# Square of the GELU argument written back to the matmul's PSUM bank, with the next VectorE step reading it there

## Chip, cores and metric

One core of one Trainium2 chip. The metric is the device time of one execution in microseconds (us). Lower is better. A trace covers one profiled execution, and its span runs from the first to the last instruction, about 1.7 us less than the device time. Each execution has a state: fast, or slow, where the granted clock or the time shows a disturbed run.

Engines: PE is TensorE's matmuls, PEld its weight loads, DVE VectorE, ACT ScalarE, POOL GpSimd, SP the engine that issues most DMAs.

## The reference, cut to what matters

```python
def reference(...):
    g = sigmoid((x * gate_w).sum(-1))              # gate
    a = A_ref(x, wq, wk, wv, wo, beta)             # attention in 4 segments, 16 heads, with a memory;
                                                   # beta goes through a sigmoid too
    b = B_ref(x, w1, b1, w2, b2)                   # layer norm, then an MLP over the token axis
    return g * a + (1 - g) * b

def B_ref(x, w1, b1, w2, b2):                      # x: 1 x 2048 x 448
    h = layernorm(x)
    u = einsum('bsd,sf->bdf', h, w1) + b1          # f = 1792
    u = gelu(u, approximate=True)                  # 0.5 u (1 + tanh(sqrt(2/pi) (u + 0.044715 u^3)))
    y = einsum('bdf,fs->bds', u, w2) + b2
    return y.transpose(0, 2, 1)
```

## The kernel before

The kernel builds a list of operations with their reads and writes, and five texts give the order of each engine. Waits follow from the two. `name:n` in the text stands for n consecutive matmuls of a group, `name=4` for the PSUM bank that the group takes. Banks 0 to 3 belong to the attention scores. Banks 4 to 7 rotate among all other matmul groups. A group gets its bank when every operation that names it in `buse(b)` has run.

The first MLP matmul makes 14 tiles of 128 x 448, each followed by five steps:

```python
# mm1(ft), the tile ft, scratch half q = ft % 2
op("PE", ...)            # 16 matmuls into bank b, named u{ft}-0 .. u{ft}-15
op("ACT", lambda e: e.activation(gg[:, q, :], bank(b)[:, 0:D], ACT.Square, bias=b1s[:, ft : ft + 1],
                                 scale=math.sqrt(GC)),
   **buse(b), reads=[bres(b), R_bias], writes=[R_gg[q]], name=f"gsq{ft}", ...)      # GC u^2
op("ACT", lambda e: e.activation(vh[:, q, :], bank(b)[:, 0:D], ACT.Identity, bias=b1h[:, ft : ft + 1], scale=0.5),
   **buse(b), reads=[bres(b), R_bias], writes=[R_vh[q]], name=f"gvh{ft}", ...       # u/2, on ACT or DVE
op("DVE", lambda e: e.scalar_tensor_tensor(gg[:, q, :], gg[:, q, :], 1.0, vh[:, q, :], op0=ALU.add, op1=ALU.mult),
   reads=[R_gg[q], R_vh[q]], writes=[R_gg[q]], name=f"garg{ft}", ...)               # (1 + GC u^2) u/2
op("ACT", ... ACT.Tanh on gg[:, q, :] ..., name=f"gth{ft}")
op("DVE", ... (gg + 1) * vh -> uT[:, ft, :] ..., name=f"gelu{ft}")
```

A tile of the full 128-column form is split in four 32-column strips when a stretch between attention groups is short:

```python
def mm(e, out, w, x, split, **kw):
    if not split:
        return e.matmul(out, w, x, ...)
    for q in range(0, 128, 32):
        last = e.matmul(out[q : q + 32], w[:, q : q + 32], x, ...)
    return last
```

The softmax here doesn't subtract the row's maximum and nothing guards it: scores larger than these inputs give would overflow.

Of the kernel before, what the change touches and what calls it, by code (L numbers as in the profile page):

```python
# [5 lines left out]
ACT = mybir.ActivationFunctionType  # L6
ALU = mybir.AluOpType
# [5 lines left out]
D = 448  # L13
# [288 lines left out]
def pool_cost(n):  # L302
# [7 lines left out]
        warm fill0 fill1 fill2 trx1_0=4 trx1_1=5 trx0_0=6 fill3 gtr trx0_1=7 fill4 fill5 v03t v03s v03a v03b v03c  # L310
        k0a=45 v03d k0c k0b=67 q0a k0d q0b q0d q0c v67a=54 sc0_0 v67c k1a=67 k1c sc0_1 k1b=45 k1d q1a=67 sc0_2 q1c
        q1b=45 q1d sc0_3 u0-0=6 u1-0:2=7 u0-1:2 u1-2:2 pv0=4 u0-3 sc0_4 u1-4 u0-4 u1-5 btr=5 u2-0=4 u1-6 u0-5:2 u2-1:2
        u1-7 u3-0=5 u0-7 u3-1 sc1_0 u3-2:2 u2-3 u0-8:2 u2-4 u0-10 u1-8:2 u3-4 u1-10 sc1_1 u0-11 u1-11 u3-5 u1-12
        u0-12:2 u1-13 u0-14 u1-14 u0-15 u2-5 u1-15 u2-6:2 u3-6 u2-8 u3-7:2 sc1_2 u3-9 u5-0=6 u2-9 u3-10:2 u2-10:2 u5-1
        pv1=7 sc1_3 u5-2 u2-12 u5-3 u2-13 u4-0=7 u5-4 u4-1:5 u3-12 u4-6 u2-14:2 u4-7 u5-5 sc1_4 u4-8 u3-13 u4-9 u5-6
        u3-14:2 u5-7:2 u6-0=4 u5-9 u4-10:2 u6-1 u4-12:2 u6-2 u4-14 sc2_0 u7-0=5 u5-10 u4-15 u5-11 u7-1:2 u6-3:2 u7-3
        u5-12:2 u7-4 sc2_1 u7-5 u5-14 u7-6:3 pv2=7 u5-15 u6-5 u7-9 u6-6:3 u7-10 sc2_2 u6-9 mst0=7 u6-10:2 pv3=6 u7-11
        u6-12 u7-12 sc2_3 u7-13 u8-0:2=7 u7-14 u9-0=6 u6-13 u9-1:2 u6-14 u8-2 u7-15 u8-3 sc2_4 u6-15 u8-4 u9-3 u8-5
        u9-4 u8-6:2 u9-5 pv4=5 u9-6 sc3_0 u9-7 u8-8:2 u9-8 u8-10 mem4=4 u9-9 u8-11 u9-10:4 u8-12:2 u9-14:2 u8-14:2
        k2a=45 sc3_1 k2c k2b=67 k2d sc3_2 q2a=54 q2b=67 q2c q2d sc3_3 v96a=45 v96b=67 v96c v96d sc3_4 u11-0:4=4 mem6=5  # L320
        u10-0:3=7 u11-4 u10-3 pv6=6 u10-4 u11-5 pv5=5 sc4_0 u10-5:3 u13-0=5 u10-8 u11-6:2 u10-9 u13-1 mem5=6 u11-8
        u10-10 sc4_1 u10-11:2 u11-9 u10-13 u13-2 u10-14 u11-10 u13-3 u10-15 u11-11:3 u13-4 u11-14:2 u13-5 sc4_2
        u12-0:6=6 pv7=7 u12-6 u13-6 u12-7 sc4_3 mst1=4 u12-8 u13-7:2 mem7=7 u13-9 u12-9 u13-10 u12-10 sc4_4 u13-11
        u12-11 u13-12 u12-12:3 wo2=4 u12-15 wo3=7 u13-13:3 wo0~2=4 wo1=7 sc5_0 k3a=64 k3b=57 k3c k3d sc5_1 v14a=46
        pv8=5 v14c pv9=7 wo5=5 mem9=4 sc5_2 q3a=76 q3b=54 q3c q3d sc5_3 y0-0:5=7 y1-0:2=6 y0-5 y3-0:2=4 y1-2 y3-2:2
        mem8=5 y0-6 y1-3 y3-4 sc5_4 y3-5:2 y0-7 y3-7 y0-8:2 y1-4:2 y3-8:2 y0-10 sc6_0 y3-10 y0-11:2 y3-11 wo4=5 y1-6
        y3-12 y1-7 y0-13 sc6_1 y1-8:2 y3-13 y1-10:2 mem11=5 wo6=7 y1-12:2 y4-0=5 sc6_2 pv11=4 y4-1:2 y2-0=6 y4-3
        y2-1:2 y4-4 pv10=4 y4-5 sc6_3 y2-3 y4-6 y2-4 y4-7:2 mem10=7 y4-9 y5-0:2=4 y2-5:2 sc6_4 y2-7 y5-2 mst2=7 y2-8:2
        y5-3:3 y2-10 y4-10 y5-6 sc7_0 y2-11 y5-7 y2-12 y6-0=7 y5-8:3 y2-13 y6-1 y4-11 y6-2 y5-11 y4-12 sc7_1 y5-12
        y4-13 y6-3 pv12=6 y5-13 wo7=5 sc7_2 y6-4:4 y7-0:4=5 y6-8 mem12=6 y6-9 y7-4:4 mem13=4 y6-10 y7-8:2 sc7_3 pv13=6  # L330
        y6-11:3 wo9=4 y7-10 sc7_4 y7-11:2 mem14=6 y7-13 wo8=4 pv14=7 wo10=6 wo11=5 pv15=4 y8-0:2=7 y9-0:2=5 y8-2
        y9-2:3 mem15=6 y8-3 y9-5:2 y8-4:4 y9-7 y8-8:2 y9-8:2 y11-0=6 y10-0:2=4 y9-10 y11-1 y10-2 y8-10:2 y9-11 y11-2
        y8-12:2 y11-3 y10-3 y9-12:2 y11-4 y10-4 y11-5:2 y10-5 y11-7:2 y10-6:2 y11-9 y10-8 y11-10:2 y10-9:2 y11-12
        y10-11 y11-13 y10-12:2 wo12=7 wo14=6 wo13=4 y13-0=5 wo15=7 y15-0=6 y13-1 y15-1 y13-2:2 y15-2 y13-4:2 y14-0:4=4
        y15-3 y13-6:2 y12-0:2=7 y14-4:3 y12-2 y15-4 y13-8 y14-7 y15-5:2 y14-8 y13-9 y12-3 y14-9:3 y12-4 y13-10 y15-7
        y14-12 y12-5 y13-11 y15-8 y13-12 y15-9:2 y13-13 y12-6:4 y14-13 y15-11 y12-10 y15-12:2 y12-11:3 y15-0~2=5
        y15-1~2 y15-2~2 y15-3~2 y15-4~2 y15-5~2 y15-6~2 y15-7~2 y15-8~2 y15-9~2 y15-10~2 y15-11~2 y15-12~2 y15-13~2
    """,
    "ACT": """
        ldx2 ldwv1 ldwv2 xTcp0_10 xTcp0_00 cpv0 cpv1 cpv2 gt0 gt1 cpv3 gt2 cpk0_0 ek0_0 gt3 cpk0_3 ek0_1 cpk0_2 cpv4  # L340
        cpq0_1 gt4 cpq0_3 tb exp0_0=2 gt7 gt6 cpk1_0 exp0_1=3 cpk1_2 cpq1_3 exp0_2=4 cpq1_1 exp0_3=0 cpv5 gt5 eq1_0
        exp0_4=1 eq1_1 exp1_0=5 ek0_2 exp1_1=6 eq1_2 gsq0 gsq1 ek0_3 exp1_2=2 gth0 exp1_3=3 eq1_3 gth1 gsq2 exp1_4=0
        gsq3 gth2 ek1_1 exp2_0=1 gsq4 gth3 exp2_1=4 gsq5 ek1_0 gvh5 exp2_2=5 gth5 gth4 exp2_3=6 ek1_3 gsq7 exp2_4=0
        gsq6 gth7 gvh6 exp3_0=2 gth6 ek1_2 gsq9 gsq8 gvh8 exp3_1=3 cpk2_0 cpk2_3 cpq2_3 exp3_2=1 cpq2_1 cpv8 gt8
        exp3_3=4 cpv9 gt9 gt10 ek2_1 gt12 gth8 eq2_0 gt11 exp3_4=7 exp4_0=2 gth9 exp4_1=3 eq2_1 gsq10 gsq11 exp4_2=0
        ek2_0 exp4_3=5 gth11 gth10 exp4_4=6 ag2 eq2_3 gsq12 gsq13 gvh12 gvh13 ag1 exp5_0=1 gth12 cpk3_0 cpk3_3 cpq3_3
        exp5_1=4 cpv14 gt14 eq2_2 gt15 ag5 gth13 exp5_2=7 cpq3_0 ek2_3 cpq3_1 gt13 exp5_3=2 ek2_2 eq3_0 exp5_4=3
        exp6_0=0 ag4 eq3_1 exp6_1=5 eq3_2 exp6_2=6 exp6_3=2 exp6_4=3 exp7_0=1 exp7_1=4 ag7 exp7_2=7 eq3_3 exp7_3=0 ag9
        exp7_4=5 ag8 ag11 ag10 ag14
    """,  # L350
    "DVE": """
        ob0 bns2 bns1 xTcp0_11 gw bna1 xTcp0_01 bns0 padk0 padx0 padk1 padx1 bna2 bns3 bna0 padq3 padq1 bna3 padq2
        bns6 cpk0_1 ln1 bns7 bns5 bns4 ln0 bna6 mk0_0 bna4 bna7 cpq0_2 cpq0_0 bna5 bns11 bns15 cpv7 cpv6 ln2 ln3 bns8
        omgh cpk1_1 mk0_1 bna8 ln5 ln4 ln7 cpk1_3 ln6 bns12 bns9 cpq1_0 oc0 bna11 bns10 bna15 cpq1_2 bna12 phk0_0
        bna10 bna9 phk0_1 ta0 bns13 b1c bna13 bns14 b2c mo0 ln9 ln11 bna14 b1h ln8 gcol1 ln10 oc1 rec0 oc2 ln12 ln13
        ln15 ln14 mq1_0 mk0_2 phk0_2 b1s mq1_2 gh gvh0 gvh1 garg1 mk0_3 oc3 mg0 garg0 ta1 phk0_3 gelu0 mq1_1 oa0 rec1
        phq1_1 mo1 gvh2 gelu1 garg2 gcol0 oa1 gvh3 ot0 gelu2 mk1_1 mg1 garg3 phk1_1 gvh4 mo2 mg2 garg4 gelu3 ta2 rec2
        garg5 msta0 mk1_0 oa2 ta3 ot1 gelu5 mq1_3 mo3 gelu4 phk1_0 gvh7 mg3 garg7 phq1_0 mstc0 gelu7 mk1_3 garg6 tm4
        ta4 gelu6 rec3 gvh9 eps4 phq1_2 phk1_3 cpk2_1 rec4 oa3 cpk2_2 om4 oa4 mk1_2 phq1_3 cpq2_0 cpq2_2 ot3 ot2 omg0
        garg8 cpv10 cpv12 cpv11 phk1_2 tm6 mk2_1 eps6 ot4 phk2_1 ta5 ta6 garg9 tm5 gelu9 eps5 gelu8 rec5 gcol2 oa5 om5  # L360
        b2g0 gvh10 rec6 gvh11 mq2_0 om6 garg11 ta7 phq2_0 msta1 omg2 garg10 tm7 gelu11 mq2_1 gelu10 mstc1 omg1 oa6
        eps7 rec7 ag3 ot5 ag0 oa7 b2g1 garg12 phq2_1 mk2_0 om7 cpk3_1 cpk3_2 ot6 ot7 ta8 cpv15 ta9 garg13 tm9 phk2_0
        mq2_2 gelu12 phq2_2 gelu13 eps9 rec9 cpv13 mq2_3 om9 cpq3_2 phq2_3 tm8 eps8 mk2_3 mq3_0 phk2_3 mk2_2 oa9 b2g2
        rec8 om8 phk2_2 fin0 tm11 fin3 fin1 oa8 eps11 ta11 rec11 ag6 ta10 phq3_0 tm10 eps10 rec10 oa11 om10 msta2
        gcol3 ot8 omg3 mq3_1 om11 mq3_2 phq3_1 oa10 phq3_2 fin2 fin4 b2g3 ot9 mstc2 ot10 ta12 ot11 fin5 tm12 tm13
        eps12 rec12 mq3_3 oa12 om12 ta13 fin6 tm14 eps13 fin7 rec13 ta14 oa13 om13 eps14 phq3_3 rec14 ot12 tm15 ta15
        eps15 rec15 oa15 oa14 om14 om15 ot13 fin8 ot15 ot14 fin11 fin10 fin9 ag12 ag13 ag15 fin13 fin14 fin15 fin12
        fin15~2
    """,
    "POOL": """  # L370
        z3_0 id0 id1 mhalf z3_1 v0 v1 padq0 vpe0 rstd0 vpe4 wo0 rstd4 mask0_1_1 maskg0 mask0_0_0 mask0_1_3 mask0_2_2
        mask0_2_2~2 vpe8 mask0_3_0 rstd8 vpe12 rstd12 mask1_1_1 mask0_4_1 mask0_4_3 mask1_0_0 mask1_3_0 mask1_2_2
        mask1_4_1 mask1_2_2~2 mask2_0_0 mask1_1_3 mask2_1_1 mask1_4_3 mask2_1_3 mask2_2_2 mask2_2_2~2 mask3_0_0
        mask2_4_1 mask3_1_1 mask3_2_2 mask2_3_0 mask3_1_3 mask3_2_2~2 o4 mask2_4_3 mask3_4_1 mask3_4_3 mask3_3_0
# [17 lines left out]
def build_kernel(nc, X, WQ, WK, WV, WO, BETA, W1, B1, W2, B2, GW, OUT):  # L392
# [24 lines left out]
    def bank(b):  # L417
        return ps[:, b.bank if isinstance(b, Bank) else b, :]

    def bres(b):  # L420
        return b.res if isinstance(b, Bank) else R_bank[b]
# [4 lines left out]
    def buse(b):  # L426
        return {"use": (b,)} if isinstance(b, Bank) else {}
# [823 lines left out]
```

## Time and profile before

| | kernel before |
|---|---|
| median device time, first 3 runs | 174.0 us (173.86 to 174.17) |
| span of the profiled run | 170.9 us, granted clock 1.000 |
| busy: TensorE / VectorE / ScalarE / GpSimd | 166.1 / 144.2 / 127.0 / 68.6 us |
| whole matmuls recorded / strip matmuls | 404 / 508 |

(The trace has 411 weight loads for the whole matmuls, so 7 of their records are missing.) TensorE is busy to 97%, so the question for any edit elsewhere is whether TensorE waits less. The profiled run of before happened to be a quick one: its device time is 172.65, 1.3 us under the median, so spans are compared only with care.

### The profile page before, as it was taken

What the parts mean: (1) busy time and instruction counts of PE and PEld (TensorE: products, weight loads), DVE (VectorE), ACT (ScalarE), POOL (GpSimd) and SP (SyncE); (2) the same over time, 40 slices, a digit from 0 to 9 for tenths busy, and PEclk for the clock granted to TensorE, in tenths of its full rate; (3) what the DMA queues carried; (4) which work ended last, traced back from release to release, by engine and by line L of the source; (5) the groups of instructions that cost most, each with busy time, mean ns of one, the idle gap of its engine ahead of it and who ended that gap; (6) DMA issues with size and microseconds to landing.
All of it is one profiled execution on the core that took longest, in us unless ns stands there. A gap on an engine that the chain in (4) does not pass through costs nothing.

```text
span 170.9 us, 4757 instructions
## 1 busy us (share of the span) xinstructions
PE 166.1 (97%) x1953; PEld 80.0 (47%) x1960; DVE 144.2 (84%) x324; ACT 127.0 (74%) x154; POOL 68.6 (40%) x98
## 2 busy tenths in 40 slices
PE   7999999999999999999999999999999999999994
PEld 3444334444445443445454445444554455555552
DVE  2889999879897899899999999996898999977115
ACT  3469999898999999998999999989767786001000
POOL 8043285352635103384242461156826956150000
PEclk9999999999999999999999999999999999999999
DMA  5999994555563885299326000815920099735103
GB/s 176 293 207 337 293 292 99 109 152 148 127 176 69 125 226 130 50 275 229 76 77 186 0 11 21 227 42 47 252 78 29 14 245 293 211 94 171 57 0 107
DMA packets 49733, 24.57 MB, mean 144 GB/s; under 512 B 14240, under 2 KB 49472, under 8 KB 49712
## 3 DMA queue, kind: packets, MB, share of 16 engines
q1 hardware_dynamic: 49024, 23.70, 54.9%
q10 hardware_dynamic: 688, 0.57, 1.1%
q8 instruction: 15, 0.25, 0.6%
q14 instruction: 6, 0.05, 0.1%
HBM read 18.76 MB, written 2.36 MB: 124 GB/s over the span
## 4 chain that ended last, share of the span: by engine, by line
PE 82%; ACT 6%; DVE 4%; POOL 3%; DMA 2%; issue 2%; ACTq 0%
PE t L284 38%; PE t L711 20%; PE t L286 12%; PE t L973 6%; PE t L1011 4%; ACT t L982 3%; DMA t<-in_A_x_dram 2%; POOL t L985 2%; ACT t L1087 1%; POOL t L1042 1%; DVE t L1093 1%; DVE t L806 1%; DVE t L1095 1%; PE t L683 1%; ACT t L791 1%
## 5 line engine op out<-in xcount | busy, mean ns | idle before, releaser
L982 ACT ACTIVATE t<-t 128x2048 bf16<-128x2048 f32 x40 | 75.1, 1878 | 8.1 <-PE t L973 7.9
L284 PE MATMUL t<-t 128*128 128x448 bf16 (+2 forms) x404 | 78.5, 347 | 0.7 <-DVE t L793 0.4
L985 POOL TENSOR_SCALAR_AFFINE_SELECT t<-t 128x512 bf16<-128x512 bf16 x64 | 42.5, 683 | 48.3 <-ACT t L982 47.8
L284 PEld LDWEIGHTS t<-t 128*128 128x128 bf16 x411 | 37.8, 98 | 37.2 <-issue 4.4
L711 PE MATMUL t<-t 64*128 64x512 bf16 (+1 forms) x308 | 35.4, 367 | 0.5
L286 PE MATMUL t<-t 128*32 128x448 bf16 (+1 forms) x508 | 28.8, 354 | 0.0
L1042 POOL TENSOR_TENSOR t<-t 128x448 bf16<-128x448 f32 x12 | 15.6, 1305 | 23.6 <-DVE t L1038 6.8
L711 PEld LDWEIGHTS t<-t 64*128 64x128 bf16 x308 | 15.2, 94 | 17.9 <-PE t L711 3.2
L1118 DVE SCALAR_TENSOR_TENSOR t<-t 128x448 bf16<-128x448 f32 (+2 forms) x17 | 10.6, 643 | 9.3 <-PE t L284 8.6
L1067 ACT ACTIVATE t<-t 128x448 bf16<-128x448 f32 x10 | 7.2, 726 | 13.2 <-PE t L284 11.6
L286 PEld LDWEIGHTS t<-t 128*32 128x32 bf16 x508 | 12.3, 96 | 9.0 <-issue 1.9
L973 PE MATMUL t<-t 28*128 28x512 bf16 (+3 forms) x256 | 15.8, 301 | 0.3
L1048 DVE STREAM_TRANSPOSE t<-t 128x512 bf16<-128x512 bf16 x16 | 10.9, 691 | 1.1 <-POOL t L1042 1.1
L1011 PE MATMUL t<-t 128*32 128x512 bf16 (+3 forms) x256 | 11.5, 300 | 0.0
L916 DVE BATCH_NORM_STATS2 t<-t 128x6 f32<-128x448 bf16 x16 | 9.3, 607 | 2.6 <-DMA t<-in_A_x_dram 2.6
L973 PEld LDWEIGHTS t<-t 28*128 28x128 bf16 x256 | 4.5, 92 | 14.6 <-ACT t L982 7.1
L1027 DVE STREAM_TRANSPOSE t<-t 128x512 f32<-128x512 f32 x16 | 11.1, 698 | 0.2
L1025 DVE STREAM_TRANSPOSE t<-t 128x512 f32<-128x512 f32 x12 | 8.5, 712 | 2.3 <-PE t L284 0.9
L1095 DVE SCALAR_TENSOR_TENSOR t<-t 128x448 f32<-128x448 f32 x14 | 9.1, 646 | 1.0 <-ACT t L1090 0.9
L1100 DVE SCALAR_TENSOR_TENSOR t<-t 128x448 bf16<-128x448 f32 x14 | 8.9, 638 | 0.4 <-ACT t L1098 0.4
L1011 PEld LDWEIGHTS t<-t 128*32 128x32 bf16 x256 | 6.4, 96 | 5.8 <-issue 1.0
L1087 ACT ACTIVATE t<-t 128x448 f32<-128x448 f32 x14 | 8.6, 643 | 0.2 <-DVE t L1100 0.2
(73 smaller groups left out, 162.9 us busy)
## 6 DMA issues: line engine op xcount, KB each, us to landing
t<-in_B_w_dram SPq DMA_DIRECT2D x7, 1024.0 KB, 6.5
t<-in_B_w_dram SPq DMA_DIRECT2D x8, 896.0 KB, 5.9
out_dram<-t SPq DMA_DIRECT2D x15, 112.0 KB, 1.8
t<-in_A_x_dram SPq DMA_DIRECT2D x3, 448.0 KB, 4.4
t<-in_A_wo_dram SPq DMA_DIRECT2D x4, 98.0 KB
t<-in_A_wk_dram SPq DMA_DIRECT2D x1, 336.0 KB, 4.4
t<-in_A_wq_dram SPq DMA_DIRECT2D x1, 336.0 KB, 4.4
spare_heads<-t SPq DMA_DIRECT2D x8, 32.0 KB
```

Source lines behind the costliest of these rows:

```text
L284: return e.matmul(out, w, x, skip_group_check=True, **kw)
L286: last = e.matmul(out[q : q + 32], w[:, q : q + 32], x, skip_group_check=True, **kw)
L711: last = e.matmul(bank(o["b"])[:, 0 : o["n"]], o["w"](r, c), o["x"](r, c), start=first, stop=end, skip_group_check=True)
L973: last = e.matmul(bank(hl)[:, c0 : c0 + w], kT[r, hg, s * 512 + j * 128 : s * 512 + j * 128 + 128], qT[r, hg, s * 512 + 128 * j : s * 512 ...
L982: op("ACT", lambda e: e.activation(pslot(g), ps[:, 0:4, :], ACT.Exp, scale=SCALE), reads=R_bank[0:4], writes=[g.res], take=g, name=f"exp{p ...
L985: op("POOL", lambda e, c0=c0: e.affine_select(pslot(g)[:, :, c0 : c0 + 128], pslot(g)[:, :, c0 : c0 + 128], pattern=[[0, 4], [1, 128]], co ...
L1011: last = e.matmul(bank(cb)[32 * hl : 32 * hl + 32, 128 * j : 512], vaug[:, 4 * s + j, 32 * h : 32 * h + 32], pslot(P_fill[u // 2][f])[:, h ...
L1027: dv(lambda e: e.transpose(t2[:, 0, :], bank(cb)[:, 0:512]), [bres(cb)], [R_tt[tb][0]], "ta", 630, use=(cb,))
L1042: op("POOL", lambda e: e.tensor_tensor(o3, n3[0], n3[1], op=ALU.add), reads=R_tt[tb], writes=[R_ob[tb]], name=f"o{u}", cost=1280, port=Tru ...
L1048: dv(lambda e: e.transpose(oT[:, hg, s * 512 : s * 512 + 512], o), [R_ob[tb]], qres(hg, s), "ot", 635)
L1095: op("DVE", lambda e: e.scalar_tensor_tensor(gg[:, q, :], gg[:, q, :], 1.0, vh[:, q, :], op0=ALU.add, op1=ALU.mult), reads=[R_gg[q], R_vh[ ...
L1118: op("DVE", lambda e: e.scalar_tensor_tensor(outst[:, p, c0:c1], bank(b)[:, 0 : c1 - c0], omg[:, T : T + 1], ag(T)[:, c0:c1], op0=ALU.mult ...
```

## The change

The square no longer goes through the scratch in SBUF, and the VectorE step reads one operand from PSUM. (The scratch keeps its size, since the VectorE step still writes its result there.) The square now overwrites the bank, so it must follow the other reader of the bank, and the bank stays taken through the VectorE step. All five order texts are new as well. The core of the diff:

```diff
-        op("ACT", lambda e: e.activation(gg[:, q, :], bank(b)[:, 0:D], ACT.Square, bias=b1s[:, ft : ft + 1],
-                                         scale=math.sqrt(GC)),
-           **buse(b), reads=[bres(b), R_bias], writes=[R_gg[q]], name=f"gsq{ft}", ...)
         op("ACT", lambda e: e.activation(vh[:, q, :], bank(b)[:, 0:D], ACT.Identity, ...), name=f"gvh{ft}", ...)
+        op("ACT", lambda e: e.activation(bank(b)[:, 0:D], bank(b)[:, 0:D], ACT.Square, bias=b1s[:, ft : ft + 1],
+                                         scale=math.sqrt(GC)),
+           **buse(b), reads=[bres(b), R_bias], writes=[bres(b)], name=f"gsq{ft}", ...)
-        op("DVE", lambda e: e.scalar_tensor_tensor(gg[:, q, :], gg[:, q, :], 1.0, vh[:, q, :], ...),
-           reads=[R_gg[q], R_vh[q]], writes=[R_gg[q]], name=f"garg{ft}", cost=535, port=True, ...)
+        op("DVE", lambda e: e.scalar_tensor_tensor(gg[:, q, :], bank(b)[:, 0:D], 1.0, vh[:, q, :], ...),
+           **buse(b), reads=[bres(b), R_vh[q]], writes=[R_gg[q]], name=f"garg{ft}", cost=560, ...)
 ...
 "SP":        # order of the loads, start only
-        ldx0 ldwv0 ldgw ldgwb ldwk=0 ldwk0 ldb1 ldbeta ldwq=1 ldwq0 ldx4 dtx1_0 dtx1_1 ldb2 ldx8 ldx12 ldw1_0 ldw1_1
+        ldx0 ldwv0 ldgw ldgwb ldwk=0 ldwk0 ldwq=1 ldwq0 ldx4 dtx1_0 dtx1_1 ldx12 ldb2 ldx8 ldb1 ldbeta ldw1_1 ldw1_0
 ...          # the other four texts, 150 lines, cut
```

## The prediction

> **What bounds the kernel now.** I read the busy table and the slices first, then TensorE's own waits, then its timeline, then the groups of the GELU lines, and last the timeline of the two engines that feed TensorE.
>
> The busy table and the TensorE row of the forty slices:
>
> ```profile
> PE 166.1 (97%) x1953; PEld 80.0 (47%) x1960; DVE 144.2 (84%) x324; ACT 127.0 (74%) x154; POOL 68.6 (40%) x98
> ...
> PE   7999999999999999999999999999999999999994
> ```
>
> TensorE is busy in every slice but the first and the last. Busy is not the same as streaming, because ends are modelled and a matmul that sits in the pipe counts as busy. So I rebuilt the stream. Two pieces of TensorE's timeline, one where nothing waits and one with the longest wait:
>
> ```profile
> 46.26 0.40 PE L973 MATMUL t<-t 28*128 28x512 bf16 x4
> 46.59 2.44 PE L284 MATMUL t<-t 128*128 128x448 bf16 x12
> 48.96 0.40 PE L973 MATMUL t<-t 28*128 28x384 bf16 x8
> ...
> 60.87 1.12 PE L284 MATMUL t<-t 128*128 128x448 bf16 x5
> 62.37 1.86 PE L284 MATMUL t<-t 128*128 128x448 bf16 x9 [0.37 <-DVE t L793]
> ```
>
> Twelve 448-column matmuls cost 12 x 448/2.4 = 2.24 us at full clock (it is 1.000 all through), 2.26 with about 2 ns each; start to start they take 48.96 - 46.59 = 2.37. The missing 0.11 us is the step into the score group (four 28-row tiles at once). The step out costs the same: 46.59 - 46.26 = 0.33 for 512/2.4 = 0.21 us of columns. Each step into or out of a score group therefore costs about 0.11 us. At 60.87 five matmuls need 0.94 us and the next begins after 1.50: 0.56 us of true wait.
>
> Adding columns over all matmul groups gives about 155 us of streaming (a few records are missing). The text of the order has 80 steps into or out of score groups, 80 x 0.11 = 9 us. The first projection begins at 5.5 and the last matmul's result leaves in the final 2.4 us of the 170.9. That sum, 155 + 9 + 5.5 + 2.4, already reaches the span within its error. Counting only the excess over streaming and over 0.11 us per step, piece by piece through the timeline, leaves about 3 us of true waits after the start-up, none over 0.6 us. This is all that any change off TensorE can win in the middle.
>
> The GELU lines, the groups by line:
>
> ```profile
> L1095 DVE SCALAR_TENSOR_TENSOR t<-t 128x448 f32<-128x448 f32 x14 | 9.1, 646 | 1.0 <-ACT t L1090 0.9
> L1100 DVE SCALAR_TENSOR_TENSOR t<-t 128x448 bf16<-128x448 f32 x14 | 8.9, 638 | 0.4 <-ACT t L1098 0.4
> L1087 ACT ACTIVATE t<-t 128x448 f32<-128x448 f32 x14 | 8.6, 643 | 0.2 <-DVE t L1100 0.2
> L1098 ACT ACTIVATE t<-t 128x448 f32<-128x448 f32 x14 | 8.0, 586 | 0.7 <-DVE t L1095 0.6
> L1093 DVE TENSOR_SCALAR t<-t 128x448 f32<-128x448 f32 x9 | 6.0, 670 | 1.3 <-ACT t L1087 1.3
> ```
>
> L1087 is the square, L1093 (L1090 on ScalarE) the half-scaled argument, L1095 the step that will read PSUM, L1098 the tanh, L1100 the last product. Their exposed waits are 1.3 + 1.0 + 0.4 + 0.2 + 0.7 = 3.6 us, but of VectorE and ScalarE, not of TensorE. Those engines matter only in so far as they are late for TensorE. Two pieces of VectorE's timeline, for its true cost per instruction:
>
> ```profile
> 47.87 0.63 DVE L1095 SCALAR_TENSOR_TENSOR t<-t 128x448 f32<-128x448 f32 x1
> 48.41 0.69 DVE L795 SCALAR_TENSOR_TENSOR t<-t 128x512 bf16<-128x512 bf16 x1
> ...
> 45.59 0.68 DVE L1093 TENSOR_SCALAR t<-t 128x448 f32<-128x448 f32 x1
> 46.19 0.70 DVE L1048 STREAM_TRANSPOSE t<-t 128x512 bf16<-128x512 bf16 x1
> ```
>
> From one start to the next, the SBUF step takes 48.41 - 47.87 = 0.54 us and a step of the same 448 columns out of PSUM 46.19 - 45.59 = 0.60. The recorded durations, 0.63 and 0.68, overlap with the successor.
>
> **What the Trainium skill says.** "Perfetto Trace Analysis", section "Optimizing Scalar/DVE Operations", gives an access overhead of about 60 ns for VectorE on SBUF and 125 on PSUM, and about 93 for ScalarE on SBUF and 51 on PSUM. The VectorE pair agrees with the trace: 448/0.96 + 60 = 527 against 0.54 us, and 448/0.96 + 125 = 592 against 0.60 us. "ScalarE: Activation LUTs", in the note on placement in "Step-by-step", says that PSUM is the lower-latency destination for ScalarE. No instruction of the kernel before writes PSUM from ScalarE, so the trace doesn't test it; the square into SBUF is 643 ns. "SBUF — State Buffer", section "Who interferes with whom", says that a VectorE instruction with two SBUF inputs contends with a GpSimd one that reads SBUF, and one with a single SBUF input doesn't. The trace agrees as far as it goes: L1095 has a median of 618 ns and a longest of 1036, and the GpSimd mask at L985 a median of 637 and a longest of 1296. "PSUM — Partial Sum Buffer", section "PSUM bank collisions raise a hardware error", says that two engines may not touch one bank and quadrant at once. The kernel orders such readers already, so square and half-scaled argument never overlapped, in either version.
>
> **The change, part by part.**
>
> Square into PSUM: 14 instructions, the same 448 columns read from PSUM with the same pointer bias. The issue-to-issue time is set by the read side, about 0.52 us in ScalarE's timeline; I expect it unchanged. Recorded duration may fall from 643 to about 600 (the skill's 93 against 51); at 14 x 0.04 that is 0.6 us of latency, not of ScalarE time.
>
> VectorE step out of PSUM: 14 x (0.60 - 0.54) = 0.8 us more of VectorE. Against it, contention goes: the mean of L1095 lies 646 - 618 = 28 ns above its median, 14 x 28 = 0.4 us. Net +0.4 us.
>
> Order of the two readers: the square must now come after the half-scaled argument, since it overwrites it. The sum of the two is the same. But the bank stays taken through L1095 too: 0.6 us more, plus VectorE's queue, some 1 us per bank; 14 banks, 14 bank-us. The four rotating banks offer about 4 x 79 = 316 bank-us between the first GELU matmuls at 24 and the last at 103, so 4%. This is a cost if TensorE wants the bank at that time.
>
> Scratch buffer: the square no longer writes the two-deep scratch tile, so it no longer waits for the last product two tiles earlier. That wait showed as 0.2 us on ScalarE, at 51.5.
>
> Order of all engines: this is the larger part of the diff. Counting names in the text: one half-scaled argument, one key copy, one value copy and one transpose copy go from VectorE to ScalarE, and two more weight-padding copies to GpSimd. VectorE loses about 2.5 us and ScalarE gains about 2. In the stretch from 20 to 110 us both are 80 to 100% busy, so this is a rebalance. On TensorE, by the kernel's rule for splitting a full matmul in four column strips, 162 tiles will be split in place of 127, so 35 x 4 = 140 more strip matmuls and 35 fewer whole ones. A split tile streams as fast: 28 strips at 50.80 are 7 tiles, 1.32 us of columns, and the next group begins 1.42 us later, 0.11 of it the step to scores. Steps into or out of score groups: 80 before and 80 after. Other steps: 6 before, 5 after.
>
> Sum on the path that sets the end: streaming 0, steps 0 to -0.1, start-up and final part 0, waits -0.5 out of the 3 us, with the bank held longer taking some back. I choose -0.5 us, or 174.0 - 0.5 = 173.5.
>
> **The rivals.** First, bank pressure: TensorE waits for a bank that L1095 still reads. If half of the 14 tiles cost 0.3 us, that is +2 us, 176. For it speaks that VectorE is over 90% busy in most of the stretch, so L1095 can queue. Against it, the new order was made with the longer hold in it, and gives other work between.
>
> Second, a gain of all waits: the freed scratch and the lighter VectorE take away most of the 3 us, which would give 171. For it: the longest wait, before 62.37, follows a VectorE queue of L875 and L1100. Against it: many of the small waits, like those before 15.76, 18.52 and 68.53, lie in the projections and have nothing to do with GELU, and a new order brings its own.
>
> Third, nothing: TensorE has the same columns and the same steps, the waits change places, 174.0. This is close to my own number, and I can't tell them apart from the profile alone.
>
> **Range and chances.** Being faster by over 2% needs -3.5 us, more than all the waits that I can find, so 0.02. Slower by over 2% needs +3.5 us of new waits on a stream that loses 3 now, possible only if the order fits the chip badly: 0.04. The rest is within 2%. The range 172.2 to 175.0 takes in a good third of the waits won beyond my figure, and bank pressure at about half of the first rival.
>
> **What would show it.** Right: TensorE still 97% busy, the same 40 score steps at 0.11 us, strip matmuls at 648, L1095's successor with a mean near 680 and no outliers near 1000, VectorE's busy time 2 to 3 us lower, ScalarE's 1.5 to 2.5 higher, the last long run of matmuls again about 23 us. Wrong: waits of TensorE's weight loads on the PSUM-reading step of over 1 us in all; a square that got longer rather than shorter; an end earlier by over 2 us, which would mean that the waits I took for fixed steps were not fixed.

## More of the kernel before

`tb` is the tanh of beta on ScalarE, and it needs the 4 KB load `ldbeta`.

## The result and the profile after

| | before | after |
|---|---|---|
| median device time | 173.93 us (173.60 to 174.17, 4 runs) | 174.52 us of all 4 (174.26 to 174.63 in 3 fast runs; a slow one at 178.55) |
| span of the profiled run | 170.9 us | 172.9 us, clock 1.000 |
| busy: TensorE / VectorE / ScalarE / GpSimd | 166.1 / 144.2 / 127.0 / 68.6 us | 166.9 / 144.7 / 129.0 / 68.3 us |
| whole / strip matmuls | 404 / 508 | 376 / 648 |
| first and last exponential start | 16.46 and 139.86 us | 18.67 and 141.35 us |

The ratio is 1.0031, 95% interval 1.0006 to 1.0055. A ratio here is always the mean time of one kernel's fast runs over that of the other's fast runs of the same rounds, so it is not quite the ratio of the quoted medians. Within 2%, but on the slow side.

The busy table and the GELU groups of the changed kernel (names moved by some lines: L1091 is the square, L1094 the VectorE step, L1097 the tanh, L1099 the last product, L1089 and L1086 the half-scaled argument):

```profile
PE 166.9 (97%) x2065; PEld 80.8 (47%) x2065; DVE 144.7 (84%) x317; ACT 129.0 (75%) x158; POOL 68.3 (40%) x101
```

```profile
L1099 DVE SCALAR_TENSOR_TENSOR t<-t 128x448 bf16<-128x448 f32 x14 | 9.0, 646 | 0.6 <-ACT t L1097 0.6
L1094 DVE SCALAR_TENSOR_TENSOR t<-t 128x448 f32<-128x448 f32 x14 | 8.5, 618 | 0.9 <-ACT t L1091 0.7
L1091 ACT ACTIVATE t<-t 128x448 f32<-128x448 f32 x14 | 8.4, 607 | 0.3 <-DVE t L1089 0.2
L1097 ACT ACTIVATE t<-t 128x448 f32<-128x448 f32 x14 | 7.9, 578 | 0.0
```

The changed steps got no slower. The square into PSUM has a mean of 607 ns, from 643. The VectorE step out of PSUM got shorter, 618 from 646, not longer. Exposed waits of the group are 0.6 + 0.9 + 0.3 = 1.8 us plus 1.6 at L1089, about what they were. So the loss is elsewhere. The first exponential already starts 18.67 - 16.46 = 2.2 us later, before any GELU tile. Two views of that moment, first ScalarE's timeline of the changed kernel, then TensorE's:

```profile
15.67 0.17 ACT L832 ACTIVATE t<-t 128x1 f32<-128x1 f32 x1
17.81 0.21 ACT L896 ACTIVATE t<-t 128x16 f32<-128x16 bf16 x1 [1.98 <-DMA t<-in_A_beta_dram]
18.05 0.59 ACT L758 ACTIVATE t<-t 64x512 bf16<-64x512 f32 x1
18.67 1.88 ACT L981 ACTIVATE t<-t 128x2048 bf16<-128x2048 f32 x1
```

```profile
16.34 0.74 PE L710 MATMUL t<-t 64*128 64x449 bf16 x6
18.70 1.49 PE L710 MATMUL t<-t 64*128 64x512 bf16 x10 [1.61 <-ACT t L758]
```

L896 is the tanh of beta. It stands 1.98 us, because its load was moved behind the last blocks of x, and ScalarE runs in order. Behind it waits the copy L758 of a projection out of its bank, and behind that TensorE, 1.61 us. A 4 KB load that has nothing to do with the GELU holds the engine that bounds the kernel. Issue and landing of that load, in the chain of waits of the changed kernel:

```profile
12.44 5.35 DMA t<-in_A_beta_dram
17.81 0.21 ACT t L896
18.05 0.60 ACT t L758
```

In the kernel before it was issued at 3.89 us in place of 12.44, and no wait for it is recorded. ScalarE's order differs at this point too: there the copy (L759) ran ahead of the tanh (L897), so that a late load could not have held the copy. ScalarE's timeline of the kernel before:

```profile
15.61 0.59 ACT L759 ACTIVATE t<-t 64x512 bf16<-64x512 f32 x1
16.22 0.21 ACT L897 ACTIVATE t<-t 128x16 f32<-128x16 bf16 x1
16.46 1.88 ACT L982 ACTIVATE t<-t 128x2048 bf16<-128x2048 f32 x1
```

### The profile page after: what moved, and what is told of

The parts are those of the page before. It is cut to its first block, busy times and chain, and to the rows that moved or that the text cites. A ratio compares the mean times of both kernels' runs of the same rounds, so it can differ in the third digit from the quotient of the medians.

```text
span 172.9 us, 4966 instructions
## 1 busy us (share of the span) xinstructions
PE 166.9 (97%) x2065; PEld 80.8 (47%) x2065; DVE 144.7 (84%) x317; ACT 129.0 (75%) x158; POOL 68.3 (40%) x101
## 4 chain that ended last, share of the span: by engine, by line
PE 86%; SPq 6%; DMA 3%; DVE 1%; issue 1%; ACT 0%
PE t L284 41%; PE t L286 18%; PE t L710 14%; PE t L972 7%; PE t L1010 5%; DMA t<-in_A_beta_dram 3%; SPq L535 3%; SPq L524 1%; PE t L857 1%; DVE t L929 1%; SPq L530 1%; SPq L528 0%; DVE t L1026 0%; ACT t L758 0%; SPq L561 0%
## 5 line engine op out<-in xcount | busy, mean ns | idle before, releaser
L284 PE MATMUL t<-t 128*128 128x448 bf16 (+2 forms) x376 | 72.3, 346 | 0.2
L284 PEld LDWEIGHTS t<-t 128*128 128x128 bf16 x376 | 34.6, 98 | 34.0 <-issue 3.8
L286 PE MATMUL t<-t 128*32 128x448 bf16 (+1 forms) x648 | 35.7, 354 | 0.0
L1041 POOL TENSOR_TENSOR t<-t 128x448 bf16<-128x448 f32 x12 | 15.1, 1264 | 22.2 <-DVE t L1037 13.9
L286 PEld LDWEIGHTS t<-t 128*32 128x32 bf16 x648 | 16.3, 96 | 11.7 <-issue 3.1
L1099 DVE SCALAR_TENSOR_TENSOR t<-t 128x448 bf16<-128x448 f32 x14 | 9.0, 646 | 0.6 <-ACT t L1097 0.6
L1094 DVE SCALAR_TENSOR_TENSOR t<-t 128x448 f32<-128x448 f32 x14 | 8.5, 618 | 0.9 <-ACT t L1091 0.7
L1010 PEld LDWEIGHTS t<-t 128*32 128x32 bf16 x256 | 6.8, 97 | 5.2 <-POOL t L984 0.4
L819 DVE SCALAR_TENSOR_TENSOR t<-t 128x512 bf16<-128x512 bf16 x12 | 8.9, 745 | 0.0
```

The source lines that it names most:

```text
L284: return e.matmul(out, w, x, skip_group_check=True, **kw)
L286: last = e.matmul(out[q : q + 32], w[:, q : q + 32], x, skip_group_check=True, **kw)
L1010: last = e.matmul(bank(cb)[32 * hl : 32 * hl + 32, 128 * j : 512], vaug[:, 4 * s + j, 32 * h : 32 * h + 32], pslot(P_fill[u // 2][f])[:, h ...
L1041: op("POOL", lambda e: e.tensor_tensor(o3, n3[0], n3[1], op=ALU.add), reads=R_tt[tb], writes=[R_ob[tb]], name=f"o{u}", cost=1280, port=Tru ...
```

## The experiments

Theory 1: the late beta load costs what the change loses, and the new dataflow is nearly free. Rival: the longer hold of the bank costs. Second rival: the PSUM form gains much, and something else eats it. The kernels ran on one chip with the runs of the kernel before: the first four on one, the next four on a second, the last four on a third.

### The changed kernel again

> The changed kernel once more, as the base of this call. All theories: ratio to the kernel before 1.002 to 1.006, as measured first. In its profile ScalarE should wait about 2 us before the tanh of beta and TensorE 1.6 us just after; if the load lands early in this run, the time should be lower by as much.

Measured: 174.61 us median against 173.51 of before, ratio 1.0079 (1.0056 to 1.0103). This is higher than the first 1.0031. The changed kernel hardly moved (174.52 and 174.61); the kernel before was faster on this chip. ScalarE waited 1.3 us for beta and TensorE 0.9 behind it, so the load's landing varies from run to run. This run is the base for the next three.

### Small loads early

```diff
-ldwk=0 ldwk0 ldwq=1 ldwq0 ldx4 ... ldx8 ldb1 ldbeta ldw1_1
+ldwk=0 ldwk0 ldb1 ldbeta ldwq=1 ldwq0 ldx4 ... ldx8 ldw1_1
```

> Changed kernel, with the two small loads (bias 1 and beta) put back to where the kernel before issues them, ahead of the query weights. Theory 1 (the new order delays the small beta load, ScalarE stands 2 us before the tanh of beta, TensorE behind it): ratio to the kernel before 0.990 to 0.996, the first exponential starts within 0.7 us of the kernel before's, ScalarE's wait for beta is gone. Rival (the longer hold of the PSUM bank costs): the wait for beta goes, but the time stays within 0.3 us of the changed kernel, 1.002 to 1.006. Second rival (profile changes the load's timing and the timed runs never had the wait): also 1.002 to 1.006.

Measured: 173.78 us median, ratio 1.0028 (0.9995 to 1.0061), so about 0.9 us less than the changed kernel on the same chip (1.0079 - 1.0028 = 0.0051 of 173.5). The profiled run, before its clock fell, at 21.3 us, shows no wait for beta and the first exponential at 17.04 us. The direction is theory 1's, the size less than it expected. The ratio lies in the 1.002 to 1.006 that both rivals gave, but not within their 0.3 us of the changed kernel on the same chip. The edit also puts two issues ahead of the query weights, which can cost something of its own.

### Square in SBUF, new order

```diff
-e.activation(bank(b)[:, 0:D], bank(b)[:, 0:D], ACT.Square, ...), writes=[bres(b)]
+e.activation(gg[:, q, :], bank(b)[:, 0:D], ACT.Square, ...), writes=[R_gg[q]]
-e.scalar_tensor_tensor(gg[:, q, :], bank(b)[:, 0:D], 1.0, vh[:, q, :], ...), **buse(b)
+e.scalar_tensor_tensor(gg[:, q, :], gg[:, q, :], 1.0, vh[:, q, :], ...)
```

> Changed kernel's order on all engines, but the square goes to the SBUF scratch again and the next VectorE step reads it there (reader order of the bank as in the changed kernel). Theory 1 (dataflow is nearly free at TensorE's end): within 0.4 us of the changed kernel, ratio to before 1.001 to 1.008, square back to a mean of 640 ns from 607. Rival, bank pressure costs: faster than the changed kernel by over 0.5 us, ratio under 1.000. Rival, PSUM gains much: slower by over 0.7 us, ratio over 1.008.

Measured: 176.88 us median, ratio 1.0211 (1.0183 to 1.0240). Against the changed kernel this is 1.0211/1.0079 = 1.013, or 2.3 us. My theory's second half falls: the dataflow is not nearly free, the PSUM form is worth 2.3 us in this order. The square is back at 634 ns. But the large difference is in the VectorE step. The group in this kernel, and one of its slow instances beside GpSimd's mask:

```profile
L1094 DVE SCALAR_TENSOR_TENSOR t<-t 128x448 f32<-128x448 f32 x14 | 11.1, 817 | 1.6 <-ACT t L1091 1.4
```

```profile
53.57 0.63 DVE L1094 SCALAR_TENSOR_TENSOR t<-t 128x448 f32<-128x448 f32 x1
...
57.04 1.05 DVE L1094 SCALAR_TENSOR_TENSOR t<-t 128x448 f32<-128x448 f32 x1
```

```profile
55.37 2.25 POOL L984 TENSOR_SCALAR_AFFINE_SELECT t<-t 128x512 bf16<-128x512 bf16 x3 [5.58 <-ACT t L981]
```

The mean is 817 ns against 617 with the operand in PSUM, 14 x 0.2 = 2.8 us of VectorE. The instance at 57.04 took 1.05 us, and three masks ran from 55.37 to 57.62; the one at 53.57 had none beside it and took 0.63. Laid against GpSimd's instructions, all 14 instances of this trace show the same: six took 970 to 1249 ns, and each of them overlaps a GpSimd instruction (five a mask, one the sum L1041); the other eight took at most 626, and seven of them had no GpSimd instruction beside them. With one operand in PSUM, 10 of the 14 instances of the first trace overlap a GpSimd instruction, and the longest instance is 625 ns (626 in the second trace). So with two operands in SBUF the step can be slowed by a GpSimd instruction beside it, and with one it was not.

### Both edits

> Both edits: early small loads, square to SBUF, the changed kernel's order otherwise. Against the run with early small loads alone it isolates the dataflow with the 2 us wait out of the way. Theory 1: within 0.4 us of that run (0.990 to 0.998). Bank pressure: faster than that run by over 0.5 us. PSUM gains: slower than that run by 0.5 us or more.

Measured: 176.27 us, ratio 1.0184 (1.0144 to 1.0224). Against the small loads alone 1.0184/1.0028 = 1.0156, or 2.7 us. The gain of the PSUM form is there with the beta wait reduced too.

### New dataflow in the old order

The five pairs of square and half-scaled argument that both run on ScalarE change places, and the VectorE steps of tiles 8, 9, 10 and 13 come earlier, since else the program would wait for itself. Operations as in the change.

```diff
-gsq5 ek1_0 gvh5 ... gsq9 gsq8 gvh8 ... gsq12 gsq13 gvh12 gvh13        # ACT
+gvh5 ek1_0 gsq5 ... gsq9 gvh8 gsq8 ... gvh12 gvh13 gsq12 gsq13
-cpk2_1 ... garg8 ... garg9 ... garg11 ta7 ... garg10 ... cpk3_1 ... garg13   # DVE
+garg9 garg8 cpk2_1 ... garg10 garg11 ta7 ... garg13 cpk3_1
```

> Kernel before with only the change of the dataflow: square written back to the bank, read from there. Its own order is kept except that the half-scaled argument comes ahead of the square where both are on ScalarE, and four of the VectorE steps come earlier, since else the program would wait for itself (a bank not yet free). Theory 1 (dataflow neutral, order matters): 0.995 to 1.006 of the kernel before. Bank pressure: over 1.006, with TensorE waits at the tiles of the GELU. PSUM gains: under 0.995.

Measured: 187.06 us, ratio 1.0775 (1.0743 to 1.0807), 13 us slower than before. Theory 1 falls here entirely, bank pressure holds. Its TensorE timeline:

```profile
37.35 0.37 PE L286 MATMUL t<-t 128*32 128x448 bf16 x4
40.60 2.81 PE L286 MATMUL t<-t 128*32 128x448 bf16 x28 [2.88 <-DVE t L1070]
```

L1070 is the VectorE step. A group that wants the bank stands 2.88 us until that step has read it. In all, TensorE's recorded waits on L1070 come to 3.0 + 2.9 + 2.9 + 1.7 = 10.5 us. Such a pause has a second price. Two stretches of this kernel (busy times of PE, PEld, DVE, ACT and POOL, then the granted clock, here 1.00 and 0.66, then DMA):

```profile
30.00:40.00 10.00, 7.72 (x57) 3.31 (x55) 7.43 (x26) 8.10 (x10) 3.97 (x6) 1.00 0.57 141
40.00:45.00 5.00, 4.40 (x52) 1.92 (x53) 1.38 (x4) 2.00 (x3) 0.00 (x0) 0.66 0.25 61
```

From 40 to 45 us TensorE had a mean clock of 0.66: half the clock from 40.18 to 43.60, 3.4 us, which by itself costs 1.7 us. (One fast execution of this kernel kept 1.000 and took 185.68 us.) The Trainium skill, "TensorE: Matmul & The Clock Gate", section "Why this matters for your kernels", warns of idle gaps over about 3 us between bursts; this one is 40.60 - 37.35 - 0.19 = 3.1 us from the end of the streaming, and agrees. The record does not make 3 us a limit, though. In the trace of the longer hold below, a pause of 2.4 us, counted in the same way, brought the same 3.4 us of half clock, while pauses of 2.1 us (here, before 54.16) and 2.2 us (there, before 59.12) brought none.

### Beta load late in the old order

```diff
-ldwk0 ldb1 ldbeta ldwq=1 ... ldx8 ldx12 ldw1_0
+ldwk0 ldwq=1 ... ldx8 ldx12 ldb1 ldbeta ldw1_0
```

> Kernel before with the two small loads issued where the changed kernel has them, after the last block of x. Theory 1 (the late beta load is what costs): 1.006 to 1.013, that is 1 to 2.2 us slower, with a ScalarE wait for beta of 1 to 2 us before the first exponential. Rival: within 0.3 us of the kernel before, 0.998 to 1.002.

Measured: 173.86 us against 173.29, ratio 1.0033 (1.0017 to 1.0050), 0.6 us slower. ScalarE waited 0.7 us for beta in its trace, not the 1 to 2 expected. The ratio falls between the two expectations. That the late load costs time is confirmed by itself in the other kernel, at a third of the size of the longest wait seen. Here the copy still ran ahead of the tanh, and TensorE waited only 0.46 us, behind the first exponential.

### Tanh of beta two places later

```diff
-gt4 tb cpq0_3 exp0_0=2 gt6 gt7
+gt4 cpq0_3 exp0_0=2 tb gt6 gt7
```

> Changed kernel, loads untouched, but the tanh of beta stands two places later in ScalarE's order, behind the first exponential. Theory 1: the wait is hidden under the exponential, ratio to before 0.990 to 0.997, unless VectorE, which needs the result, then waits. Rival: unchanged, 1.002 to 1.006.

Measured: 173.56 us against 173.29, ratio 1.0005 (0.9984 to 1.0027). No wait for beta is left in the trace, the span is 171.2 us and the last exponential starts at 139.60, 0.3 before that of the kernel before. The change without this wait is as fast as the kernel before, within 0.3%. (The unedited changed kernel was not run on this chip.) That is better than unchanged (1.002 to 1.006 was the rival's), and worse than I expected of theory 1.

### Bank held through the tanh

```diff
-e.activation(gg[:, q, :], gg[:, q, :], ACT.Tanh, ...), reads=[R_gg[q]]
+e.activation(gg[:, q, :], gg[:, q, :], ACT.Tanh, ...), **({} if ft in (8, 9, 12, 13) else buse(b)), reads=[R_gg[q]]
```

> Changed kernel with early small loads, and the bank of 10 of the 14 GELU tiles given free only after the tanh instead of after the VectorE step, some 1 us later (four tiles can't be held longer in this order without the program waiting for itself). A test of how much the hold of a bank costs. Theory 1 (the hold is nearly free in this order): within 0.4 us of the run with early small loads. Bank pressure: slower than that run by 0.7 us or more, with new TensorE waits before GELU tiles.

Measured: 184.33 us, ratio 1.0595 (1.0544 to 1.0646). Against the small loads early this is 1.0595/1.0028 = 1.0565, or 9.8 us for ten tiles, about 1 us each. Here bank pressure holds: TensorE now waits on the tanh, 2.9 + 2.7 + 1.4 = 7.0 us as recorded, and the mean clock falls to 0.991. (The two runs are from different chips, and one fast execution at clock 1.000 took 182.13 us, so part of the 9.8 is the clock.) In both orders a hold that the order was not made for is dear.

### Deeper scratch for the SBUF form

What does the SBUF form lose in the new order? Either the block by GpSimd, or the wait for the two-deep scratch, which the PSUM form doesn't have.

```diff
-gg = sb([128, 2, D], F32)          # and gg[:, q, :] with q = ft % 2
+gg = sb([128, 4, D], F32)          # and gg[:, ft % 4, :]
```

> The changed kernel's order with the square in an SBUF scratch, as in the earlier run that took 1.0211 of the kernel before, but the scratch four deep in place of two, so that no square waits for the product two tiles back. Theory 2a (what the SBUF form loses in this order is the VectorE step blocked by GpSimd, since both operands are in SBUF: it had a mean of 817 ns there): still 1.016 to 1.024, mean of that step still over 750 ns. Theory 2b (it loses by the wait for the scratch): back to 1.004 to 1.011, as the changed kernel.

Measured: 176.68 us, ratio 1.0181 (1.0156 to 1.0206). The VectorE step still has a mean of 818 ns. So the scratch is not the main cause; the ratios differ by 0.3%, and the two intervals overlap (they are from different chips). By elimination, and by the step's own times and overlaps, the cause is the block by GpSimd. I did not run a kernel that takes the masks off GpSimd in this order, so it stays an inference that these 2.8 us of VectorE make the 2.3 us of the kernel.

### Old order, half-scaled argument first, square in SBUF

The kernel of the new dataflow in the old order, with the two lines of the SBUF form put back. It keeps the order of the readers and drops the hold.

> The kernel that put the new dataflow into the old order (1.0775 of the kernel before), same order text and same order of the two readers, but the square in SBUF again, so the bank is free after the square and not after the VectorE step. Theory 3a (the hold of the bank through the VectorE step costs it): most of the 13 us vanish, 1.00 to 1.02. Theory 3b (the square, now behind the half-scaled argument on VectorE, costs it: ScalarE waited 7.5 us there): most remain, over 1.05, and ScalarE still waits over 5 us for the half-scaled argument.

Measured: 178.62 us, ratio 1.0309 (1.0263 to 1.0356). Neither expectation holds; both causes have a part. Of the 7.75% that the new dataflow costs in the old order, 3.1% (5.4 us) remain with the new order of readers and the moved VectorE steps alone, where ScalarE still waits 5.9 us for the half-scaled argument on VectorE. The other 4.7% (8 us, between two chips, and with it the half clock) come with the hold, and TensorE's waits on the VectorE step, 10.5 us, are gone without it.

### A pointer in place of the constant

I had taken the extra 0.06 us of an instruction out of PSUM for the price of PSUM, and the result contradicted it.

```diff
-e.scalar_tensor_tensor(gg[:, q, :], bank(b)[:, 0:D], 1.0, vh[:, q, :], ...)      # tanh of beta later as well
+e.scalar_tensor_tensor(gg[:, q, :], bank(b)[:, 0:D], onecol, vh[:, q, :], ...)   # onecol: [128, 1] of 1.0
```

> Changed kernel with the tanh of beta two places later, and the constant 1.0 of the VectorE step as a per-partition pointer operand (a column of ones) in place of an immediate; same result. A look at the step's own time. If the 0.06 us that I had put down to reading PSUM belongs to a pointer operand, the step's start to the next start goes from 0.535 to about 0.60 us, its duration from 615 to about 680 ns. If not, both stay. The whole time should stay within 1 us of 173.6.

Measured: one look, 173.86 us. The group:

```profile
L1095 DVE SCALAR_TENSOR_TENSOR t<-t,const-float32-1.0 128x448 f32<-128x448 f32 x14 | 9.2, 678 | 0.9 <-ACT t L1092 0.7
```

Mean 678 against 619 ns with the constant, and 0.60 us from start to start against 0.535 (medians of the unstalled ones). The 0.06 us belongs to the per-partition pointer operand. The kernel before had shown it: L1038 has both tensors in SBUF and a pointer, and takes 0.60 us from start to start; L1040, another operation on the same columns without a pointer, 0.535.

### Candidate for a best version

```diff
-"DVE": bns3 xTcp0_10 ... bna1 ob0 bna0        # tanh of beta two places later as well
+"DVE": ob0 bns3 xTcp0_10 ... bna1 bna0
```

> Candidate for a best version: changed kernel, tanh of beta two places later, and the clearing of the output scratch put back to the front of VectorE's order, where VectorE waits for x anyway (0.48 us). If VectorE is late in the first 20 us: 0.2 to 0.5 us faster than with the tanh alone, ratio to before 0.996 to 0.999. If not: 0.999 to 1.002.

Measured: 173.57 us against 173.51, ratio 0.9992 (0.9972 to 1.0012). It can't be told from the kernel before, nor from the version with the later tanh alone. No version beat the kernel before by more than the interval.

### The four combinations side by side

| ratio to the kernel before | old order | new order |
|---|---|---|
| square in SBUF | 1 (1.0309 with the bank's readers exchanged) | 1.0211 |
| square in PSUM | 1.0775 (order changed where it had to be) | 1.0031 and 1.0079; 1.0005 with the tanh of beta later |

Each order is good for the dataflow it was made for. Within the new order the PSUM form gains 1.3%; the new order itself, late beta load included, loses 2.1% with the old dataflow. Together that is the 0.8% of the changed kernel on that chip, and without the wait for beta it is nothing that can be told from 0.

## Why the prediction was right or wrong

The time, 174.52, lies in the range and in the class of highest chance. The centre, 173.5, had the wrong sign: -0.5 was foreseen, +0.6 came. Both terms that decided the sum, waits and start-up, were wrong, and the time fell in the range because each error was small. That part is luck. The third rival, "nothing", came nearest. By the steps:

- Bound by TensorE, some 3 us of waits to be won, over 2% out of reach. The bound held, and no version was faster than the kernel before by more than its interval. TensorE is again busy to 97%, the strip matmuls number 648 as counted, and the last run of matmuls takes 23.9 us in both traces. The budget behind the 3 us doesn't close: 155 + 9 + 5.5 + 2.4 and 3 us of waits are 174.9, against a span of 170.9. TensorE works from 2.06 us on, so part of the start is counted twice. The rate of 2.4 columns per ns is the trace's own: whole matmuls of 448 columns start 0.189 us apart.
- "Start-up and final part 0" failed. I had counted the moved copies but not followed the moved loads to their first user. The tanh of beta waited 1.98 us in the first trace, 1.3 in the second. Putting the load back brought the ratio from 1.0079 to 1.0028 on one chip; moving the tanh behind the copy and the exponential gave 1.0005 on another. The count of copies was short by one as well: three weight-padding copies go to GpSimd (padk1, padx0, padq1), not two.
- "Waits -0.5" is not seen. Without the beta wait the kernel equals the one before, so the term is 0 within some 0.2%.
- "VectorE step out of PSUM +0.8 us" failed. The step takes 0.535 us from start to start from PSUM, as from SBUF. The 0.06 us was a pointer operand. My reading "The VectorE pair agrees with the trace" came from rows that differed in two things at once.
- "Contention goes", 0.4 us, was right in kind, and its size depends on the order: 28 ns an instruction in the old order, 200 in the new one. In the new order this is, by the inference above, the term that carries the gain of the PSUM form.
- The bank's longer hold as a cost was named as a rival and then set against the new order "made with the longer hold in it". Both were right: 8 us in the old order; in the new one TensorE's weight loads waited on the VectorE step once in each trace, 0.4 and 0.6 us, under the 1 us that was to show the prediction wrong.
- VectorE's busy time was to fall by 2 to 3 us. It rose by 0.5. The removed copies are gone, but others grew: the layer-norm step L929 from a mean of 389 to 471 ns (16 of them, +1.3 us; longest 422 before, 1122 after) and L819 from 672 to 745 (+0.9). The one L929 of 1.00 us, at 12.27, ended at 13.27, and GpSimd's clearing of a buffer had run from 12.19 to 13.14. The other slow one, of 1.12 us at 29.28, overlaps such a clearing too (L615), and the 14 without one took at most 398 ns. That the two block each other there is my reading of the overlap; no run isolates it. L929 has a single tensor input, in SBUF: the prediction's "one with a single SBUF input doesn't" is wider than the page, which says it only for instructions outside its 2-port modes.
- ScalarE +1.5 to 2.5: +2.0 measured. The square at about 600 ns: 607. In the same order and on the same chip it took 634 into SBUF and 607 into PSUM, so the trace agrees with the note on placement that PSUM is the lower-latency destination. Where nothing held the next instruction, it began after 0.52 us in both forms, as expected.

The views, VectorE's and GpSimd's timelines of the changed kernel, for L929 in the last but one point:

```profile
12.27 1.00 DVE L929 TENSOR_SCALAR t<-t 128x448 bf16<-128x448 bf16 x1
...
13.46 0.38 DVE L929 TENSOR_SCALAR t<-t 128x448 bf16<-128x448 bf16 x1
```

```profile
12.19 0.95 POOL L606 MEMSET t<- 128x1024 uint32 x1
```

## What to carry to other kernels

Where a hand-made or searched order fits one dataflow, test an edit of the dataflow in the old order and in the new one; the price of the edit depends on the order, here +7.75% in the old one and -1.3% in the new one. In an in-order engine follow each moved load, however small, to its first user and to what stands behind that user. Before you put a cost down to a memory, find two rows that differ in that memory alone.

## What the Trainium skill lacked or had wrong

- "Perfetto Trace Analysis", section "Optimizing Scalar/DVE Operations": its 125 ns for VectorE on PSUM is not borne out here. A step of 448 columns with one operand in PSUM takes 0.535 us from start to start, 448/0.96 + 68 ns. A 512-column cast out of PSUM (L806 of the kernel before) takes 0.61, some 512/0.96 + 74. Both are nearer to its 60 ns for SBUF. (The rate of 0.96 columns per ns fits the traces: 448 columns in 0.535 us and 512 in 0.602, L820.)
- No page that I read gives VectorE's price of a per-partition pointer operand. It is about 0.06 us: 0.535 to 0.60 us with PSUM, and 0.535 against 0.60 with both tensors in SBUF.
